# The two wide matmuls of the first attention scores, split into query halves around K's last transposes

## The chip, the cores and the metric

The kernel runs on one core of one Trainium2 chip. The metric is the device time of one execution in microseconds (us). A ratio below is the mean time of one kernel's runs over that of the other's in the same rounds, so it is not quite the ratio of the medians that are quoted.

## The reference, cut to what matters

```python
xn = layernorm(x)                                    # x: 2048 x 640
q = (xn @ wq).reshape(B, Sq, 32, 192)                # 32 heads, head size 192
scores = einsum("bhqd,bhkd->bhqk", q, k_cache) * 192 ** -0.5
o = einsum("bhqk,bhkd->bhqd", softmax(scores), v_cache)
g = silu((silu(x @ w1) * (x @ w3)) @ w2)
return x + (o.reshape(B, Sq, -1) @ wo) * g
```

The kernel walks over 1024 steps of (head, block of 512 queries, pair of key blocks). A step takes scores on PE, exponentials on ACT and the product with V on PE. (PE is TensorE, which multiplies matrices and writes the results to PSUM; ACT is ScalarE, DVE is VectorE, POOL is GpSimd, and SP issues most of the transfers.) The change concerns the very first step, where the pipeline is still being filled.

## The kernel before

The head start brings the first 512 rows of x and K of head 0, normalises x, transposes both on PE, projects the first queries and starts the stream (cut to the end of that function):

```python
    project_first()              # queries of block 0, in two halves of 256 (L391 to L396)
    turn_k0(pk1, 1, (2, 3))      # K's last eight transposes on PE (L271)
    copy_k0(nc.scalar.copy, pk1, 1, 1)     # their copy from PSUM, on ACT (L277)
    scores(0)
    shift_first()                # DVE copies of query halves (L400, L401)
    shift_k0()                   # DVE copy of K rows (L281)
    scores(1)
    ln_stats(1, 0)               # layer norm of the second block, on DVE ...
    ...
    ln_turn_dma(1, 0)            # ... its transposes, by DMA (L360)
```

The first two steps of the scores have a form of their own. Two matmuls on all 128 rows do the work of two rounds, and one round of two half-row matmuls follows:

```python
    if (h, qb) == (0, 0) and p < 2:
        rounds = rounds[2:]
        nc.tensor.matmul(st2[:, 0:512],    lhsT=KW[:, 0, ks], rhs=qA[:], start=True, stop=False)   # L483
        nc.tensor.matmul(st2[:, 512:1024], lhsT=KW[:, 4, ks], rhs=qA[:], start=True, stop=False)   # L484
    for r, (ka, qa, kb, qb2) in enumerate(rounds):
        nc.tensor.matmul(st2[:, 0:512], lhsT=ka, rhs=qa, ...)       # L487, rows 0 to 63
        nc.tensor.matmul(st2[:, 512:1024], lhsT=kb, rhs=qb2, ...)   # L488, rows 64 to 127
    ...                          # exponentials on ACT (L493), in two parts for step 0
```

`swap_halves(0)`, issued when the first block is transposed, copies that block with its partition halves exchanged (xnS). The projection of head 1 (L424, at pair 3 of the first block) uses PE as two row tiles, that is two arrays of 64 of the 128 rows, and its second row tile begins with this copy. The DMA transposes of the second block feed that block's projection of head 0 (L410, at pair 5).

## Time and profile before

| | before |
|---|---|
| time | 1938.26 us (3 runs, 1937.99 to 1938.29) |
| PE busy, granted clock | 99%, 0.999 |
| ACT busy | 61% |
| first exponential starts | 14.08 us |
| waits of the value products for ACT, whole span | 0.6 us |

A timeline row reads: start, busy us, engine, line, operation, output<-input, shapes, count, and in brackets the idle time before it with its releaser. PEld is the loading of PE's weights. A PE row's start is what to read, since the ends of matmuls are modelled.

### The profile page before, as it was taken

To read this page: it belongs to the slowest core of one execution; us is meant where nothing else is said; L and a number is where in the kernel's file an instruction comes from. 1 tells how busy PE (TensorE), PEld (TensorE's weight loads), DVE (VectorE), ACT (ScalarE), POOL (GpSimd) and SP (SyncE) were. 2 spreads that over 40 slices of the span, in tenths; PEclk is the share of its full clock that TensorE was granted. 3 is DMA by queue.
4 is the path that set the end of the run, shared out by engine and by line. 5 is a ranking of instruction groups with operands and counts; after the bars stand their busy time and mean duration, and the time that the engine had idled before them with its cause. 6 is when DMAs were issued, how large, how long until landed. Compare 5 with 4: busy or idle time off the path is not lost.

```text
span 1936.4 us, 59669 instructions
## 1 busy us (share of the span) xinstructions
PE 1926.6 (99%) x27273; PEld 1315.6 (68%) x27281; DVE 654.6 (34%) x997; ACT 1180.0 (61%) x1279; POOL 282.5 (15%) x501
## 2 busy tenths in 40 slices
PE   9999999999999999999999999999999999999998
PEld 6666666666666666666666666666666666577776
DVE  7333333333333333333333333333333334521111
ACT  6677676767676767776777777677767677210000
POOL 3111111111111111111111111111111110000000
PEclk9999999999999999999999999999999999999999
DMA  8643433323333434363434343434334220937783
GB/s 181 129 101 67 98 68 86 84 62 88 59 90 61 100 63 97 68 162 69 101 66 100 69 101 69 101 64 101 69 69 96 58 68 2 260 69 137 151 152 62
DMA packets 394643, 178.98 MB, mean 92 GB/s; under 512 B 341616, under 2 KB 382832, under 8 KB 394384
## 3 DMA queue, kind: packets, MB, share of 16 engines
q1 hardware_dynamic: 371136, 125.32, 31.6%
q0 software_dynamic: 19472, 45.71, 10.0%
q8 instruction: 215, 3.52, 0.8%
q10 hardware_dynamic: 3776, 4.06, 0.7%
q14 instruction: 44, 0.36, 0.1%
HBM read 52.82 MB, written 27.79 MB: 42 GB/s over the span
## 4 chain that ended last, share of the span: by engine, by line
PE 99%; DVE 1%; DMA 0%; ACT 0%; issue 0%; DVEq 0%; ACTq 0%
PE obank L519 35%; PE st L487 34%; PE ps L424 14%; PE ps_s L111 11%; PE ps_f L731 3%; PE ps_gu L705 1%; PE st L488 1%; PE ps L410 0%; DVE stats L316 0%; DMA x_all<-in_A_x_dram 0%; PE ps L391 0%; PE pst L354 0%; PE pk L271 0%; DVE xn L346 0%; ACT pT L493 0%
## 5 line engine op out<-in xcount | busy, mean ns | idle before, releaser
L493 ACT ACTIVATE pT<-st 128x1024 bf16<-128x1024 f32 (+1 forms) x1025 | 1046.1, 1021 | 250.2 <-PE st L488 234.0
L519 PEld LDWEIGHTS <-pT 64*128 64x128 bf16 x16384 | 711.3, 94 | 242.3 <-ACT pT L493 0.6
L519 PE MATMUL obank<-vt,pT 64*128 64x193 bf16 x16384 | 849.7, 243 | 0.0
L487 PE MATMUL st<-qC,KW 64*128 64x512 bf16 x2046 | 605.6, 376 | 0.1
L528 DVE COPY osum<-obank 128x772 f32<-128x772 f32 x128 | 123.1, 962 | 787.1 <-PE obank L519 787.1
L488 PE MATMUL st<-qB,KW 64*128 64x512 bf16 x1024 | 385.0, 376 | 0.0
L487 PE MATMUL st<-qA,KW 64*128 64x512 bf16 x1022 | 384.3, 376 | 0.1
L488 PE MATMUL st<-qC,KW 64*128 64x512 bf16 x1022 | 384.3, 376 | 0.0
L488 PE MATMUL st<-qA,KW 64*128 64x512 bf16 x1022 | 384.3, 376 | 0.0
L487 PEld LDWEIGHTS <-KW 64*128 64x128 bf16 x3068 | 278.5, 94 | 153.7 <-issue 2.1
L424 PE MATMUL ps<-xnT,W 64*128 64x512 bf16 x1280 | 297.2, 376 | 0.0
L424 PE MATMUL ps<-xnS,W 64*128 64x512 bf16 x1280 | 296.0, 376 | 0.0
L488 PEld LDWEIGHTS <-KW 64*128 64x128 bf16 x3068 | 278.5, 94 | 0.5
L377 POOL DMA_DIRECT2D qC<-qA x124 | 65.4, 528 | 1283.0 <-DVE rl_all L535 1268.2
L430 ACT CAST qB<-ps 128x512 bf16<-128x512 f32 x131 | 76.7, 585 | 228.2 <-PE ps L424 222.6
L111 PE MATMUL ps_s<-wo_sb,oT 128*128 128x384 bf16 (+3 forms) x1535 | 208.8, 299 | 0.1
L424 PEld LDWEIGHTS <-W 64*128 64x128 bf16 x2560 | 122.9, 94 | 121.4 <-issue 0.2
L111 PEld LDWEIGHTS <-oT 128*128 128x128 bf16 x1536 | 148.4, 98 | 60.4
L529 DVE TENSOR_TENSOR osum<-osum,obank 128x772 f32<-128x772 f32 x128 | 122.7, 959 | 13.4
L536 DVE TENSOR_TENSOR ostage<-osum,rl_all 128x768 bf16<-128x768 f32 x128 | 122.7, 958 | 6.3 <-DMA o_scr<-ostage 1.9
L465 DVE SCALAR_TENSOR_TENSOR hT<-pt,qB 64x512 bf16<-64x512 bf16 x64 | 43.8, 684 | 197.4 <-ACT pt L464 197.4
L429 DVE CAST qA<-ps 128x512 bf16<-128x512 f32 x131 | 90.6, 692 | 25.3 <-PE ps L410 7.2
(84 smaller groups left out, 621.9 us busy)
## 6 DMA issues: line engine op xcount, KB each, us to landing
o_scr<-ostage SPq DMA_DIRECT2D x16, 1536.0 KB, 10.6
vt<-in_A_v_cache_dram SPq DMA_DIRECT2D x63, 384.0 KB, 5.9
qC<-qA POOLq DMA_DIRECT2D x248, 64.0 KB, 1.9
qC<-qB POOLq DMA_DIRECT2D x124, 64.0 KB, 2.3
wo_sb<-in_A_wo_dram POOLq DMA_DIRECT2D x1, 7680.0 KB, 36.1
W<-in_A_wq_dram POOLq DMA_DIRECT2D x32, 160.0 KB, 3.6
W<-in_B_w_dram POOLq DMA_DIRECT2D x32, 80.0 KB, 3.3
W<-in_A_wq_dram POOLq DMA_DIRECT2D x32, 80.0 KB, 3.0
```

The costliest lines, as they stand in the source:

```text
L111: nc.tensor.matmul(ps[:, 0:w], lhsT=oT[:, k, :], rhs=wo_sb[:, k, c0:c1], start=(k == 0), stop=(k == OC - 1))
L377: nc.gpsimd.dma_start(out=qC[0:64, half, :], in_=qAB[half][64:P, :])
L424: nc.tensor.matmul(ps[:, r * 512:(r + 1) * 512], lhsT=W[rows, j, :], rhs=xs[rows, j // 2, qs], start=(j == 0), stop=(j == 2 * DC - 1))
L429: a = nc.vector.tensor_copy(out=qAB[0][:], in_=ps[:, 0:512])
L430: b = nc.scalar.copy(out=qAB[1][:], in_=ps[:, 512:1024])
L487: nc.tensor.matmul(st2[:, 0:512], lhsT=ka, rhs=qa, start=r == 0 and nr == 3, stop=r == nr - 1)
L488: nc.tensor.matmul(st2[:, 512:1024], lhsT=kb, rhs=qb2, start=r == 0 and nr == 3, stop=r == nr - 1)
L493: nc.scalar.activation(out=pT2[:, c * w:(c + 1) * w], in_=st2[:, c * w:(c + 1) * w], func=ACT.Exp, scale=att_scale)
L519: nc.tensor.matmul(obanks[r][:, j * 256:j * 256 + DH + 1], lhsT=pT2[r * 64:(r + 1) * 64, t * 512 + j * P:t * 512 + (j + 1) * P], rhs=vt[r ...
L528: nc.vector.tensor_copy(out=osum[:], in_=ov[0])
L529: nc.vector.tensor_tensor(out=osum[:], in0=osum[:], in1=ov[1], op=ALU.add)
L536: nc.vector.tensor_tensor(out=ostage[:, qb * 4:qb * 4 + 4, hg * DH:(hg + 1) * DH], in0=osum[:, :, 0:DH], in1=rl.unsqueeze(2).to_broadcast( ...
```

## The change

The intent is to use PE's wait for the second query cast. The two 512-wide matmuls become four of 256. The pair for the first query half runs straight behind the projection, and the pair for the second half behind K's last transposes.

```diff
+    def half_scores():
+        KW, qA, i = loads[0]["KW"], qtiles[0, 0][0][0], early["half"]
+        early["half"] += 1
+        qs = slice(i * 256, (i + 1) * 256)
+        for b, a in enumerate((0, 4)):
+            nc.tensor.matmul(early["st"][:, b * 512 + i * 256:b * 512 + (i + 1) * 256], lhsT=KW[:, a, 0:P], rhs=qA[:, qs],
+                             start=i == 0, stop=False)
...
         project_first()
+        first_scores()
+        half_scores()
         turn_k0(pk1, 1, (2, 3))
         copy_k0(nc.scalar.copy, pk1, 1, 1)
+        half_scores()
         scores(0)
```

`first_scores` only takes the PSUM tile, and the scores of step 0 skip their two wide matmuls where that tile exists. The inserted lines shift the numbering: L484 is now the split matmul, L487/L488 are L507/L508, the exponential L493 is L513, the value product L519 is L539.

More of the change, by code (lines that the diff above doesn't have):

```diff
@@ L469, in _kernel_impl, with first_scores @@
     stream = [(h, qb, p) for h in range(H) for qb in range(NQB) for p in range(NPAIR)]
+    early = {}
+    def first_scores():
+        early["st"] = ps_st.tile([P, 1024], F32, tag="st2", name="st2")
+        early["half"] = 0
+    def half_scores():
[5 more added lines that the diff above has]
+                             start=i == 0, stop=False)
     def emit_scores(h, qb, p):
@@ L476, in emit_scores @@
         ks = slice(p * P, (p + 1) * P)
-        st2 = ps_st.tile([P, 1024], F32, tag="st2", name="st2")
+        st2 = early.pop("st", None)
+        begun = st2 is not None
+        if not begun:
+            st2 = ps_st.tile([P, 1024], F32, tag="st2", name="st2")
         rounds = [(KW[0:64, 0, ks], qA[0:64, :], KW[64:P, 1, ks], qC[64:P, 0, :]),
@@ L482, in emit_scores @@
             rounds = rounds[2:]
-            nc.tensor.matmul(st2[:, 0:512], lhsT=KW[:, 0, ks], rhs=qA[:], start=True, stop=False)
-            nc.tensor.matmul(st2[:, 512:1024], lhsT=KW[:, 4, ks], rhs=qA[:], start=True, stop=False)
+            if not begun:
+                nc.tensor.matmul(st2[:, 0:512], lhsT=KW[:, 0, ks], rhs=qA[:], start=True, stop=False)
+                nc.tensor.matmul(st2[:, 512:1024], lhsT=KW[:, 4, ks], rhs=qA[:], start=True, stop=False)
         nr = len(rounds)
```

## The prediction

> **What bounds the kernel now.** I read the page of the kernel before first (busy shares, slices, chain), then all waits of the weight loads and of PE over the whole span, then the timeline from 8 to 18 us, where the change sits, one engine at a time, and last the chain of work between 12 and 16 us.
>
> ```profile
> PE 1926.6 (99%) x27273; PEld 1315.6 (68%) x27281; DVE 654.6 (34%) x997; ACT 1180.0 (61%) x1279; POOL 282.5 (15%) x501
> PEclk9999999999999999999999999999999999999999
> PE 99%; DVE 1%; DMA 0%; ACT 0%; issue 0%; DVEq 0%; ACTq 0%
> ```
>
> The first line is busy time by engine, the second the granted clock in 40 slices, the third the chain that ended last. TensorE is busy for 99% of the span at full clock and makes up 99% of the chain. The change touches only the first 15 us of 1936, so it can win no more than the waits that stand there. The waits of the weight loads over the whole span (line, releaser, total us, times, longest) say how much that is:
>
> ```profile
> PEld L519 <- ACT pT L493: 0.6, 3, 0.2
> PEld L483 <- ACT qB L394: 0.3, 1, 0.3
> ```
>
> L483 is the first matmul of the first scores, the one that the change splits; L519 multiplies the exponentials by the values, and two of its three waits lie at 14.7 and 15.2 us. So all that is at stake is about 0.3 + 0.4 us, 0.04% of the time. What ends last in this stage is told by the timelines of PE and of ACT (start, us, line, operation, out<-in, count):
>
> ```profile
> 10.15 2.35 PE L391 MATMUL ps<-xnT,W 128*128 128x256 bf16 x20
> 12.33 0.61 PE L271 MATMUL pk<-ident_bf,kn 128*128 128x128 bf16 x8
> 13.10 0.38 PE L483 MATMUL st<-qA,KW 128*128 128x512 bf16 x1 [0.16 <-DVE qA L393]
> 13.63 0.39 PE L487 MATMUL st<-qC,KW 64*128 64x512 bf16 x1
> 14.17 0.38 PE L484 MATMUL st<-qA,KW 128*128 128x512 bf16 x1
> 14.49 0.39 PE L487 MATMUL st<-qC,KW 64*128 64x512 bf16 x1
> ```
> ```profile
> 12.98 1.01 ACT L277 COPY KW<-pk 128x1024 bf16<-128x1024 bf16 x1
> 14.08 1.08 ACT L493 ACTIVATE pT<-st 128x512 bf16<-128x512 f32 x2
> ```
> ```profile
> 12.53 0.42 DVE L393 CAST qA<-ps 128x256 bf16<-128x256 f32 x1 [0.67 <-PE ps L391]
> 12.99 0.29 DVE L396 COPY qC<-qB 64x512 bf16<-64x512 bf16 x1
> ```
>
> The reader is to see two chains that meet at the first exponential, at 14.08. On PE: the projection (L391) ends at 12.50, DVE casts its second half until 12.95, L483 starts at 13.10, L484 one slot later, near 13.31 (its record is missing; its weight load is there at 13.10), L487/L488 at 13.63 until 14.02, and the exponential follows 0.06 us later. On ACT: the eight last turns of K (L271, 12.33 to 12.94) release the copy of K's last part, 12.98 to 13.99; it stands ahead of the exponential in ACT's queue. The chain of waits for 12 to 16 us leads through the PE side. The ACT side is only 0.18 us behind it, as worked out below, and that small margin is what this prediction turns on.
>
> ```profile
> 14.73 0.28 PEld L519 LDWEIGHTS <-pT 64*128 64x128 bf16 x8 [0.15 <-ACT pT L493]
> 15.22 0.28 PEld L519 LDWEIGHTS <-pT 64*128 64x128 bf16 x8 [0.21 <-ACT pT L493]
> ```
>
> These two lines say why the start of the first exponential counts at all: its two halves, 0.59 us each and 0.50 apart, release the first value products, and PE waits for both. From 15.5 us on PE runs without a wait for ACT, and the start of the stream is set.
>
> **What the Trainium skill says.** (1) "TensorE: Matmul & The Clock Gate", Back-to-back issue gap: a warm matmul of N columns takes N/2.4 + 2.5 ns of issue, so 109 ns for 256 columns and 216 for 512. The trace agrees: the 20 matmuls of L391, 256 columns each of 272 ns, take 2.35 us, which is (2.35 - 0.272)/19 = 0.109 each. Splitting a 512-wide matmul in two is thus almost free in streaming. The same page says in its step-by-step part that matmuls stay in program order, so what is put ahead of K's turns delays them. (2) "TensorEngine Tiling (Array Packing)", Key Properties: a change of the tiling mode drains the array. The trace agrees: from L484 (all 128 rows) to L487 (64 rows) is 0.32 us at 14.17, where 0.216 would be the bare issue. (3) "ScalarE: Activation LUTs", What ACT_TABLE_LOAD costs: back-to-back activations overlap by about 93 ns. The trace agrees: the two copies of L277 at 9.57 take 1.94 us together at 1021 ns each, an overlap of 0.10. (4) "PSUM — Partial Sum Buffer", The four PSUM rules: a first matmul with the start flag clears the written marks of its whole bank, so of two groups in one bank only the one issued first may have it, and the other's first write overwrites. The change does it so (start on half 0 only). It costs no time; the value products here already rely on it, two results to a bank.
>
> **The change part by part.**
>
> It removes the two 512-wide matmuls L483 and L484 of the first scores (2 x 0.216 = 0.43 us of issue) and adds four of 256 columns (4 x 0.109 = 0.44 us). The sum of PE's work is unchanged, +0.005 us. Two weight loads are added, 0.098 us each, hidden under matmuls of 0.109 as under L391.
>
> It moves half 0 ahead of K's last eight turns. Its buffer is the one that the casts of the first projection half left at about 11.86, its query columns are from the same cast, and its K columns were copied by 11.50. It should wait for nothing and start at 12.33, where the turns start now. The turns go from 12.33 to 12.33 + 2 x 0.109 = 12.55; their last one starts 7 x 0.056 later, at 12.94, and ends with its 0.219 at 13.16 rather than 12.94. This is the price.
>
> PE's gain: half 1 needs the second cast, which doesn't move (12.95), so it starts at 13.10 like L483 now, and has 0.218 of issue instead of 0.432. L487 then starts at 13.21 + 0.11 + 0.10 for the change of mode = 13.42. It also needs the copy L396, done at 13.28, 0.14 before, which fits the 0.15 that L483 took to follow its cast. So L487/L488 come at about 13.43 rather than 13.63, and end at 13.82 rather than 14.02. By PE alone the exponential would start at 13.88: 0.20 us won.
>
> ACT's loss: its copy of K's last part starts 0.04 after the last turn, so at 13.20 rather than 12.98. The next ACT instruction can start 1.01 - 0.09 = 0.92 later: 13.90 now (which is the margin of 0.18 to 14.08), and 13.20 + 0.92 = **14.12 after**. The first exponential starts at the later of 13.88 and 14.12, so at 14.12, 0.04 us **later** than now. The first value products move from 14.73 to 14.77 and 15.22 to 15.26. The second scores get ready 0.2 us earlier on PE, but only lengthen PE's wait for the exponential. From there everything is shifted by +0.04 us, or less where a DVE chain (the normalisations of the next blocks, which the change leaves where they are) is what PE waits for, as near 34.8 us.
>
> Sum: 0.44 - 0.43 on PE is hidden in a wait, the gain of 0.20 on PE's chain is overtaken by ACT's, and +0.04 is left. 1938.26 + 0.04 = 1938.3 us.
>
> **The rivals.**
>
> PE's chain stays the bound, as the intent of the change is. Then 0.20 us is won: 1938.06. For it: the chain of waits before runs through the PE side and doesn't name ACT. Against it: the copy stands in the same queue as the exponential, 0.18 us from being the bound, and the change delays it by 0.22. A middle way, turns delayed by less because the array overlaps them with something, gives 1938.1 to 1938.3.
>
> A new wait: half 1 comes after the copy of K's last part in program order, and both touch the same K tile. If half 1 were made to wait for the copy (done at 14.21), L487 would start at about 14.60 and the exponential at 15.05, a loss of 0.95: 1939.2. Against it: L483 stands behind the same copy now and started at 13.10, in the middle of it; their columns of K don't overlap.
>
> A shift that grows or vanishes later: a start moved by some hundredths can let a transfer or a DVE step of the first head fall on another side of a PE instruction. Waits there are 0.4 us at most each (the scores at 34.81 for a cast), so some tenths to 1 us either way. The three runs before span 0.3 us, which says that the kernel itself is steady.
>
> **Range and chances.** The main way gives 1938.3, PE's way 1938.06, the false wait 1939.2. To that I add about 1 us to both sides for regrouping in the first head and for another session or chip, which three runs on one chip can't show; that is a guess. Range 1937.0 to 1939.5. Two per cent is 38.8 us, some 50 times all the waits at stake, so within 2% is as good as certain: 0.99, the rest for something that no view shows.
>
> **What would show each step.** Right: two matmuls of 256 columns at about 12.33 and two at 13.10; the turns from 12.55 to 13.16; the ACT copy at 13.20; L487 at 13.43; the first exponential at 14.12, directly behind the copy with no wait for PE; the value products' two waits grown by 0.04 and PE's own time unchanged. Wrong: a first exponential at 13.9 (PE was the bound, or the turns weren't delayed), half 0 later than 12.4 (a wait for its buffer that I haven't seen), L487 later than 13.6 (a false wait for the copy). If these times are as told and the whole differs by more than 0.5 us, the difference comes from later in the kernel, and my step "shifted by +0.04 from there" is what failed.

## The result, and the profile after

The changed kernel took 1938.11 us (median of 6 runs, 1937.93 to 1939.62), the kernel before 1938.13 (6 runs). The ratio is 1.0001, 95% interval 0.9988 to 1.0014: the same time.

The page of the changed kernel, busy time and the chain that ended last:

```profile
PE 1927.4 (100%) x27275; PEld 1316.6 (68%) x27283; DVE 654.3 (34%) x997; ACT 1179.9 (61%) x1279; POOL 282.5 (15%) x501
PE 99%; DVE 0%; ACT 0%; POOL 0%; issue 0%; POOLq 0%; DVEq 0%; ACTq 0%
```

There are two matmuls and two weight loads more. PE's busy time reads 0.8 us more than before, but 0.1 us less in the second pair of profiles below (1927.1 before, 1927.0 after), so that is scatter. The start has to be read closely. In the PE timeline of the changed kernel:

```profile
10.23 2.35 PE L391 MATMUL ps<-xnT,W 128*128 128x256 bf16 x20
12.41 0.38 PE L484 MATMUL st<-qA,KW 128*128 128x256 bf16 x2
12.63 0.61 PE L271 MATMUL pk<-ident_bf,kn 128*128 128x128 bf16 x8
13.09 0.38 PE L484 MATMUL st<-qA,KW 128*128 128x256 bf16 x2
13.41 0.38 PE L507 MATMUL st<-qC,KW 64*128 64x512 bf16 x1
```

And in its ACT timeline:

```profile
13.28 1.01 ACT L277 COPY KW<-pk 128x1024 bf16<-128x1024 bf16 x1 [0.29 <-PE pk L271]
14.18 2.01 ACT L513 ACTIVATE pT<-st 128x512 bf16<-128x512 f32 x3
```

This profile runs 0.08 us late from the first transfer on: the projection L391 starts at 10.23, not 10.15. All times from here on are therefore counted from the start of L391 in the same profile and called relative. For an example, the first exponential is at 14.18 - 10.23 = 3.95 after and 14.08 - 10.15 = 3.93 before.

| relative start, us | before | after |
|---|---|---|
| K's last transposes (PE) | 2.18 | 2.40 |
| their copy (ACT) | 2.83 | 3.05 |
| last round of the first scores (PE) | 3.48 | 3.18 |
| first exponential (ACT) | 3.93 | 3.95 |
| first value product (PE) | 4.59 | 4.61 |

PE is ready 0.30 us earlier, and the exponential comes no earlier. The chain of work from 12 to 16 us in the changed kernel shows what took over:

```profile
12.57 0.22 PE st L484 x2
12.79 0.46 PE pk L271 x8
13.25 0.02 issue
13.28 1.01 ACT KW L277
14.29 0.51 ACT pT L513
14.80 0.05 issue
14.84 1.00 PE obank L539 x16
```

The chain now leads from the inserted half through K's transposes and ACT's copy. Before, it led from the projection through DVE to PE's scores and did not touch ACT's copy:

```profile
12.53 0.42 DVE qA L393
12.99 0.30 DVE qC L396
13.31 0.30 DVE qC L400
13.63 0.39 PE st L487
```

The releaser L400 is inferred here. In the built program L487 waits for L396 alone, done at 13.29, so PE's own order set its start: 13.10, a slot of 0.22 and 0.32 for the last of the wide matmuls give 13.64. PE's gain has become a longer wait for ACT (waits of the weight loads after, to be held against 0.6 before):

```profile
PEld L539 <- ACT pT L513: 0.9, 3, 0.5
```

### The profile page after: what moved, and what is told of

Read it like the earlier page. It is cut to its first block, busy times and chain, and to the rows that moved or that the text cites. A ratio compares the mean times of both kernels' runs of the same rounds, so it can differ in the third digit from the quotient of the medians.

```text
span 1936.2 us, 59673 instructions
## 1 busy us (share of the span) xinstructions
PE 1927.4 (100%) x27275; PEld 1316.6 (68%) x27283; DVE 654.3 (34%) x997; ACT 1179.9 (61%) x1279; POOL 282.5 (15%) x501
## 4 chain that ended last, share of the span: by engine, by line
PE 99%; DVE 0%; ACT 0%; POOL 0%; issue 0%; POOLq 0%; DVEq 0%; ACTq 0%
PE obank L539 35%; PE st L507 34%; PE ps L424 14%; PE ps_s L111 11%; PE ps_f L754 3%; PE ps_gu L728 1%; PE st L508 1%; PE ps L410 0%; PE pk L592 0%; PE ps L391 0%; PE pst L354 0%; PE pk L271 0%; ACT pT L513 0%; ACT KW L277 0%; POOL W L223 0%
## 5 line engine op out<-in xcount | busy, mean ns | idle before, releaser
L513 ACT ACTIVATE pT<-st 128x1024 bf16<-128x1024 f32 (+1 forms) x1025 | 1046.1, 1021 | 250.1 <-PE st L508 234.0
L539 PEld LDWEIGHTS <-pT 64*128 64x128 bf16 x16384 | 711.2, 94 | 242.7 <-ACT pT L513 0.9
L539 PE MATMUL obank<-vt,pT 64*128 64x193 bf16 x16384 | 849.6, 243 | 0.2 <-ACT pT L513 0.2
L507 PE MATMUL st<-qC,KW 64*128 64x512 bf16 x2046 | 605.7, 376 | 0.0
L508 PE MATMUL st<-qB,KW 64*128 64x512 bf16 x1024 | 385.1, 376 | 0.0
L507 PE MATMUL st<-qA,KW 64*128 64x512 bf16 x1022 | 384.4, 376 | 0.1
L508 PE MATMUL st<-qC,KW 64*128 64x512 bf16 x1022 | 384.3, 376 | 0.0
L508 PE MATMUL st<-qA,KW 64*128 64x512 bf16 x1022 | 384.3, 376 | 0.0
L507 PEld LDWEIGHTS <-KW 64*128 64x128 bf16 x3068 | 278.6, 94 | 153.8 <-issue 1.9
L424 PE MATMUL ps<-xnT,W 64*128 64x512 bf16 x1280 | 297.2, 376 | 0.0
L424 PE MATMUL ps<-xnS,W 64*128 64x512 bf16 x1280 | 296.3, 376 | 0.0
L508 PEld LDWEIGHTS <-KW 64*128 64x128 bf16 x3068 | 278.5, 94 | 0.2
L377 POOL DMA_DIRECT2D qC<-qA x124 | 65.4, 528 | 1282.9 <-DVE rl_all L555 1268.2
L424 PEld LDWEIGHTS <-W 64*128 64x128 bf16 x2560 | 122.8, 94 | 121.3
```

The lines of the kernel that those rows point to most:

```text
L377: nc.gpsimd.dma_start(out=qC[0:64, half, :], in_=qAB[half][64:P, :])
L424: nc.tensor.matmul(ps[:, r * 512:(r + 1) * 512], lhsT=W[rows, j, :], rhs=xs[rows, j // 2, qs], start=(j == 0), stop=(j == 2 * DC - 1))
L507: nc.tensor.matmul(st2[:, 0:512], lhsT=ka, rhs=qa, start=r == 0 and nr == 3, stop=r == nr - 1)
L508: nc.tensor.matmul(st2[:, 512:1024], lhsT=kb, rhs=qb2, start=r == 0 and nr == 3, stop=r == nr - 1)
L513: nc.scalar.activation(out=pT2[:, c * w:(c + 1) * w], in_=st2[:, c * w:(c + 1) * w], func=ACT.Exp, scale=att_scale)
L539: nc.tensor.matmul(obanks[r][:, j * 256:j * 256 + DH + 1], lhsT=pT2[r * 64:(r + 1) * 64, t * 512 + j * P:t * 512 + (j + 1) * P], rhs=vt[r ...
```

## The experiments

The theory is that the first exponential starts at the later of two times, PE's last round and ACT's copy, and that the change moved the second by as much as it won on the first. The rivals are that something else in the split holds the exponential, or that the copy does not matter. All kernels gave correct results. For the kernels that were timed, every ratio to the kernel before has an interval of about plus or minus 0.0014 (2.7 us) that holds 1, so the ratios decide nothing here. Runs of one kernel spread too: in the rounds of the first four experiments the kernel before took 1937.77 to 1939.34, five of nine runs at 1939.15 or more.

### Both halves behind the transposes

```diff
-        first_scores()
-        half_scores()
         turn_k0(pk1, 1, (2, 3))
+        first_scores()
+        half_scores()
         copy_k0(nc.scalar.copy, pk1, 1, 1)
         half_scores()
```

> Both halves of the first scores stand behind K's last turns; half 0 fills the wait for the cast. Times are counted from the first matmul of the first projection (L391), where the kernel before has its first exponential at 3.93 us and the changed one at 3.95. My theory (the first exponential starts at the later of PE's scores and ACT's copy of K's last part, and the change delays the copy by 0.22): the turns go back to 2.18, the copy to 2.83, half 1 stays at 2.86 and the last pair of the first scores at 3.18; ACT is free at 2.83 + 0.90 = 3.73, PE ready at 3.63, so the exponential starts at 3.73, the first value product at 4.39 rather than 4.59 or 4.61, and the whole is 0.20 us shorter than the kernel before: 1937.9 for 1938.1. Rival 1 (PE's order is all that counts, ACT's copy doesn't matter): 3.63. Rival 2 (something else that the split brings, a wait for the buffer or for the flags, holds the exponential at about 3.95): no change against the changed kernel.

The PE timeline of this kernel, then its ACT timeline:

```profile
10.37 2.35 PE L391 MATMUL ps<-xnT,W 128*128 128x256 bf16 x20
13.00 0.61 PE L484 MATMUL st<-qA,KW 128*128 128x256 bf16 x4
13.55 0.38 PE L507 MATMUL st<-qC,KW 64*128 64x512 bf16 x1
```
```profile
13.20 1.01 ACT L277 COPY KW<-pk 128x1024 bf16<-128x1024 bf16 x1
14.11 2.01 ACT L513 ACTIVATE pT<-st 128x512 bf16<-128x512 f32 x3
```

The copy is back at 2.83, the last round at 3.18 as in the changed kernel, and the exponential at 3.74 (3.73 expected). The first value product is at 4.40, 0.19 earlier than before. Half 0 now fills exactly the time that PE waited, and delays nothing. The whole time, 1938.04 us (5 runs, ratio 0.9996, 0.9982 to 1.001), can't show 0.2 us.

### The copy on DVE, with the change and without

```diff
-        copy_k0(nc.scalar.copy, pk1, 1, 1)
+        copy_k0(nc.vector.tensor_copy, pk1, 1, 1)
```

In the changed kernel:

> The changed kernel with the copy of K's last part on DVE rather than ACT. My theory: ACT's queue is empty ahead of the exponential, so it starts when PE is ready, 3.18 + 0.39 + 0.05 = 3.62 us after the start of the first projection (3.95 in the changed kernel), the first value product at 4.28. The whole is 0.3 us shorter, unless the 0.68 us more on DVE delay the normalisations that the first head waits for. Rival 1 (the copy isn't what held the exponential): it stays at 3.95. Rival 2 (DVE is the tighter engine here): the exponential comes earlier and the total doesn't follow, or gets worse by up to 0.7.

In the kernel before, as control:

> The kernel before with the copy of K's last part on DVE rather than ACT: the control. My theory says that before, PE was the bound and ACT's copy 0.18 us behind it, so that taking the copy off ACT brings nothing: first exponential at 3.93 us from the start of the first projection, first value product at 4.59, time unchanged. Rival (the copy held the exponential already before): it starts earlier, by up to 0.2.

The ACT row of the changed kernel with this edit, then that of the kernel before with it:

```profile
13.92 2.00 ACT L513 ACTIVATE pT<-st 128x512 bf16<-128x512 f32 x3 [0.87 <-PE st L508]
```
```profile
14.26 2.00 ACT L493 ACTIVATE pT<-st 128x512 bf16<-128x512 f32 x3 [1.18 <-PE st L488]
```

L391 starts at 10.29 and 10.32 here. With the change the exponential moves from 3.95 to 3.63, and its releaser is now PE. Without the change it stays (3.94 for 3.93). The same edit is worth 0.32 us in one kernel and nothing in the other. That shows that the copy binds after the change and didn't bind before it.

The totals don't follow: 1938.29 and 1938.41 us (ratios 0.9998 and 0.9997 to the kernel before in the same rounds). Rival 2 of the first text, that DVE's extra work costs later what was won, is at least partly right. The second block's DMA transposes are issued at 18.74 rather than 18.06 us, and PE waits for what comes of them (L410, below).

### The delay repeated, in two doses

```diff
         half_scores()
+        turn_over(8)            # 36 in the other kernel: idle 128-wide matmuls
         turn_k0(pk1, 1, (2, 3))
```

> The changed kernel with eight idle matmuls of 128 columns more (as in its warm-up) between half 0 and K's last turns: twice as much delay again as half 0 makes. My theory: 8 x 0.056 = 0.45 us on the turns, so the copy at 3.50 and the exponential at 4.40 from the start of the first projection (3.05 and 3.95 in the changed kernel), the first value product at 5.06, and all of it in the whole time: 1938.55. Rival 1 (the exponential isn't bound by turns and copy): less than 0.45 on the exponential. Rival 2 (a shift of the start is taken up by slack in the first head): the exponential moves, the total doesn't.

> The changed kernel with 36 idle matmuls of 128 columns between half 0 and K's last turns: a delay large enough to be read in the whole time. My theory: 36 x 0.056 = 2.0 us on turns, copy (5.06 us from the start of the first projection), exponential (5.96) and first value product (6.62), and as PE is the bound from there on, the whole time 2.0 us longer, 1940.1. Rival (slack in the first head, where PE waits for DVE at 20 to 40 us, takes up part of it): between 0 and 1.5 us longer; then a gain of some tenths at the first exponential needn't reach the total either.

Copy and exponential on ACT with 8 (L391 at 10.28), then with 36 (L391 at 10.40):

```profile
13.77 1.01 ACT L277 COPY KW<-pk 128x1024 bf16<-128x1024 bf16 x1 [0.74 <-PE pk L271]
14.68 2.01 ACT L513 ACTIVATE pT<-st 128x512 bf16<-128x512 f32 x3
```
```profile
15.46 1.01 ACT L277 COPY KW<-pk 128x1024 bf16<-128x1024 bf16 x1 [2.30 <-DVE stats L316]
16.36 2.01 ACT L513 ACTIVATE pT<-st 128x512 bf16<-128x512 f32 x3
```

(The copy waits for PE's transposes in both. The releaser L316 in the second is a wrong inference: the transposes there run from 14.81 to 15.42.) Copies at 3.49 and 5.06, exponentials at 4.40 and 5.96, value products at 5.06 and 6.62: all as expected to 0.01 us. A delay on K's transposes is a delay on the first exponential, one for one. The 36-matmul kernel took 1940.15 us (5 runs within 0.11), against 1938.34 for the kernel before in its rounds (1937.97 to 1939.07, so no run of the one reaches the other; ratio 1.0009, 0.9995 to 1.0022). By the medians 1.8 of the 2.0 us arrived at the end. The small dose took 1938.42 (ratio 0.9998), within the spread of its neighbours, so the 0.45 us expected in its time is neither shown nor refuted.

### Both halves behind and the copy on DVE

This combines the first and the second edit.

> Both halves behind K's last turns and the copy of K's last part on DVE. My theory: with the copy off ACT's queue the delay of the turns no longer counts, so this is as the changed kernel with the copy on DVE: exponential at 3.62 us from the start of the first projection, first value product at 4.28; whole time within 0.05 us of that kernel's, 0.3 below the kernel before. Rival (the delayed turns hurt in another way than through the copy): this one is faster by up to 0.2.

The exponential is at 3.63 and the value product at 4.28, the same as with the copy on DVE alone. So the delayed transposes hurt through ACT's copy and in no other way that shows here. The time is a miss: 1939.08 us, not 0.3 below but 0.7 above the kernel before (1938.34 in the same rounds, ratio 1.0002, not told apart). The profile says where it went. L391 starts at 10.71 here, 0.3 us or more later than in any other profile, and the rest is waiting. PE rows of the projection of head 1 in this kernel:

```profile
19.10 0.38 PE L424 MATMUL ps<-xnT,W 64*128 64x512 bf16 x1
20.12 0.39 PE L424 MATMUL ps<-xnS,W 64*128 64x512 bf16 x2 [0.64 <-DMA xnS<-xnT]
```

PE reaches the projection early (relative 8.39) and then waits 1.02 us from the first row tile to the second, for the transfer of the swapped halves. That led to a look at the same place in the first profile of the kernel before and of the changed one:

```profile
18.84 0.38 PE L424 MATMUL ps<-xnT,W 64*128 64x512 bf16 x1
19.05 0.39 PE L424 MATMUL ps<-xnS,W 64*128 64x512 bf16 x2
```
```profile
18.95 0.38 PE L424 MATMUL ps<-xnT,W 64*128 64x512 bf16 x1
18.96 0.59 PE L424 MATMUL ps<-xnS,W 64*128 64x512 bf16 x2
```

Before, the second tile came 0.21 us late; after, both start together. Is that the change's doing? Two more profiles were taken to find out.

### The same two kernels again

> The kernel before, profiled once more: a measure of how far two profiles of one kernel differ. Expected: first exponential 3.93 us and first value product 4.59 after the start of the first projection again, to 0.02; the start of that projection itself (10.15 in the first profile) and the landing of the swapped halves (8.90 after it) may differ by some tenths, as they come from transfers, and if my reading is right the wait of the second row tile for the swap (0.2 us in the first profile) changes with the landing.

> The changed kernel, profiled once more. Expected: copy at 3.05, first exponential at 3.95, first value product at 4.61 after the start of the first projection again, to 0.02; start of that projection and landing of the swapped halves by some tenths from the first profile (10.23 and up to 8.73 after it). If the landing comes later than 8.72, the changed kernel shows the same wait of the second row tile as the kernel before, and the 0.2 us between the two first profiles at the second projection of head 0 is not the change's doing.

These are single runs, so their state is unknown; the clock was 1.0 and 0.999. Everything up to the first value product repeats within 0.01 us (3.93 and 4.58; 3.05, 3.95 and 4.61). The second row tile of the changed kernel doesn't repeat:

```profile
19.01 0.38 PE L424 MATMUL ps<-xnT,W 64*128 64x512 bf16 x1
19.50 0.39 PE L424 MATMUL ps<-xnS,W 64*128 64x512 bf16 x2
25.29 2.32 PE L410 MATMUL ps<-xnT,W 128*128 128x512 bf16 x9
```

This time it waited 0.49 us. The slower transfer of the swapped halves took 7.2 us from issue to landing in the first profile of this kernel and 7.8 in this one. So the 0.2 us that seemed to speak for the change is the scatter of a transfer.

### The projection of head 1 one step later, and a load issued later

The next two kernels start from the one with both halves behind.

```diff
-        if h == 0 and qb == 0 and p == 3:
+        if h == 0 and qb == 0 and p == 4:
             project(1, 0)
```

> Both halves behind K's turns, as in the first experiment, and the projection of head 1 one step later (pair 4 rather than pair 3). Its second row tile reads the copy of the normalised input with its halves swapped, whose transfer landed in the runs so far 8.5 to 9.4 us after the start of the first projection, where PE comes to it at 8.4 to 8.7 (9.2 and 10.7 in the two delayed kernels). My theory, formed after the first experiments: what is won at the first exponential is lost again to this landing and to that of the transposes of the second block (which the second projection of head 0 waits for, at 14.4 to 14.8), so the gain doesn't reach the whole. With the projection later, PE comes to it at about 9.8 and doesn't wait for the swap: no step between its two row tiles. The second projection of head 0 still waits for the transposes, at 14.4 from the start of the first projection as in the first experiment, so the whole stays within 0.15 us of that kernel: 1938.0. Rival (the swap was the only thing that took the gain): second projection at 14.2 or earlier and the whole 0.2 us shorter.

A miss. The wait for the swap is gone, but a new one stands in its place: PE comes to the transposes of the second block (L354) before DVE has normalised it. PE row, 0.73 us idle:

```profile
21.05 0.81 PE L354 MATMUL pst<-ident_bf,xn 128*128 128x128 bf16 x10 [0.73 <-DVE xn L346]
```

L410 came at 15.31 rather than 14.4, and the time was 1938.96 us (5 runs, 1938.89 to 1941.37; ratio 1.0007, 0.9994 to 1.0021). The old place of the projection had covered DVE's work, so this run doesn't settle what the swap alone is worth.

```diff
-        load_x(2)
         project_first()
...
         scores(1)
+        load_x(2, queue=nc.scalar)
```

> Both halves behind K's turns, as in the first experiment, and the load of the third block of the input (640 KB) issued behind the second exponential, at about 16.1, rather than at 13.4 us: less traffic beside the swapped halves. In all eleven profiles so far the time of the run is 1913.2 to 1913.4 us more than the start of the second projection of head 0, which follows the landing of the second block's second transpose by 0.2 us. My theory (what a run takes is set by these landings, and they by the traffic on the transfer engines): the swap lands at 8.2 us after the start of the first projection or earlier, PE's two row tiles start together at about 8.5, and the gain of 0.2 is kept up to there; the late load now lies beside the transposes, so they may land as late as now or later (14.3 to 15.0), and the time follows the second projection's start plus 1913.3 either way. Rival (landing doesn't depend on that load): swap at 8.5 to 9.2 as before, nothing else changed. A loss is likely if the load lands after 21.9, where DVE reads it.

ACT's queue issued the load at 14.82, a little before the second exponential. The two row tiles started together (18.85, relative 8.51), and the slower half of the swap took 7.0 us, landing at relative 8.4 rather than the 8.2 that was expected. That is the shortest of the profiles compared (7.0 to 7.9), but by 0.1, which is less than the scatter just seen. L410 came at 14.30, the time was 1937.86 us (ratio 0.9999, 0.9986 to 1.0013). It is the lowest median and not told apart from the kernel before, so whether the load's traffic matters stays open.

### The profiles side by side

The second projection of head 0 (L410) is the last place where they differ. All but the last two columns are relative to L391; "tile 1/tile 2" are the starts of the two row tiles of L424.

| kernel | L391 at | first exponential | value product | L424 tile 1/tile 2 | L410 | that run's time | time minus L410's own start |
|---|---|---|---|---|---|---|---|
| before | 10.15 | 3.93 | 4.59 | 8.69/8.90 | 14.69 | 1938.20 | 1913.36 |
| before, again | 10.28 | 3.93 | 4.58 | 8.69/8.99 | 14.73 | 1938.22 | 1913.21 |
| after | 10.23 | 3.95 | 4.61 | 8.72/8.73 | 14.48 | 1937.93 | 1913.22 |
| after, again | 10.29 | 3.95 | 4.61 | 8.72/9.21 | 15.00 | 1938.51 | 1913.22 |
| both behind | 10.37 | 3.74 | 4.40 | 8.51/8.53 | 14.37 | 1938.08 | 1913.34 |
| after, copy on DVE | 10.29 | 3.63 | 4.28 | 8.39/8.75 | 14.80 | 1938.29 | 1913.20 |
| before, copy on DVE | 10.32 | 3.94 | 4.59 | 8.70/9.08 | 14.86 | 1938.48 | 1913.30 |
| after, 8 idle | 10.28 | 4.40 | 5.06 | 9.17/9.17 | 14.88 | 1938.41 | 1913.25 |
| after, 36 idle | 10.40 | 5.96 | 6.62 | 10.73/10.73 | 16.38 | 1940.06 | 1913.28 |
| both behind, copy on DVE | 10.71 | 3.63 | 4.28 | 8.39/9.41 | 15.15 | 1939.24 | 1913.38 |
| both behind, later projection | 10.33 | 3.74 | 4.40 | 11.46/11.46 | 15.31 | 1938.96 | 1913.32 |
| both behind, later load | 10.34 | 3.74 | 4.40 | 8.51/8.51 | 14.30 | 1937.86 | 1913.22 |

The last column is the find. Over twelve profiles whose times differ by 2.2 us, what comes after L410 takes 1913.2 to 1913.4 us. All but 0.2 us of what these profiled runs differ by, win, loss and scatter alike, is made by the start of L410, 27 us into the span at the latest.

From the value product to L410 the profiles need 9.76 us at the least (36 idle matmuls, where the transfers have landed long before) and 10.87 in the kernel with both halves behind and the copy on DVE, whose order of work is otherwise the usual one. The excess is waiting: for the swap, and at L410 itself. L410's first weight load waits for two transfers in the built program, and the semaphores are those that the two DMA transposes (L360) count up. In ten of the twelve profiles the load starts 0.1 us after the second of them landed. In the first profile after, for instance, the second was issued at 18.06 + 2.64 - 1.20 = 19.50 and landed 5.1 us later, at 24.6, and the load starts at 24.68. In the other two, PE comes 3.2 us (36 idle matmuls) and 2.4 us (later projection) after that landing. In these two the transfer was also quicker, 3.9 and 3.6 us from issue to landing against 4.8 to 5.6 in the ten, and the transfers of head 1's queries (L377) were issued after the landing rather than before it. So this landing seems to depend on when PE gets to the projection of head 1; why was not tested.

## Why the prediction was right or wrong

The time was right: 1938.3 told, 1938.11 measured, in the range, and the class was the near-certain one. The sign of +0.04 is not confirmed by the times: 0.02 below the kernel before, with runs 1.7 us apart. The range (1937.0 to 1939.5) is wider than the scatter of the kernel before alone (1937.77 to 1939.34), so that the time fell into it says little about the mechanism; the traces have to.

- **Half 0 starts without a wait and delays the transposes by 0.22.** Right: transposes at 2.18 before and 2.40 after.
- **The copy at 13.20, the exponential at 14.12.** Right: with L391 at 10.15 these are relative 3.05 and 3.97; measured 3.05 and 3.95. Copy and exponential start 0.90 apart, not 0.92. The overlap of 0.09 that was taken from the Trainium skill's page for pairs of activations holds for a copy followed by an exponential too, and was 0.11.
- **PE's gain of 0.20.** Right in kind, too small: it was 0.30 (3.48 to 3.18). The step that failed is "it starts at 13.10 like L483 now". Half 1 started at relative 2.86, not 2.95. The reason stands in the instruction listing of the built program (before, then after; the wait for DVE before is an instruction of its own just ahead of the weight load, counted to it here):

```
233 L483 Ldweights KW [waits DVE_49,Activation_49]
234 L483 Matmult st_312<-qA,KW 128x512 [waits Activation_49]

237 L484 Ldweights KW
238 L484 Matmult st_303<-qA,KW 128x256 [waits DVE_49]
```

Before, the weight load itself waits for DVE and ACT, so load and matmul both follow the cast: 13.10, 0.15 after the cast's end. After, half 0's weight load has done that waiting, half 1's weights load early, and only the matmul waits: 13.09, 0.06 after the cast's end at 13.03. That this is the cause follows from the listing and the two lags; no run took it away alone. From half 1 to the last round it is 0.32 in the changed kernel and also with 8 idle matmuls, where L396 was done 0.48 earlier than the round, so PE's own order suffices for that stretch. But in the changed kernel DVE's copy L396, which the round needs too, ended only 0.05 before it (13.36, then 13.41): half 1 any earlier would have met that copy.

- **"The chain of waits for 12 to 16 us leads through the PE side."** Loosely read: as shown above it runs over DVE's cast and copies to L487. That ACT's copy is not in it is right, and that is what the sum needed.
- **ACT's loss overtakes PE's gain.** Right, and shown: by the chain after, by the copy on DVE (0.32 us in one kernel, nothing in the other), by the two doses, and by both halves behind (0.21 us earlier than the changed kernel).
- **"From there everything is shifted by +0.04 us", or less for a DVE chain near 34.8.** This step failed. There are two later meetings, at 18.9 and 24.7 us, where PE comes within tenths of a transfer's landing, and the two profiles of the changed kernel differ by 0.6 us in the first of these landings and by 0.5 us in L410's start. I had checked the waits for ACT only, and taken the rest for a PE without waits. The wait of 0.21 at L424 was in the profile before, in a row labelled "issue" that I passed over, and busy time hid it because the first tile's matmul was still counted. Of the rivals, the one that a shift "grows or vanishes later" by a transfer falling on another side of a PE instruction is what the traces show.
- **A false wait of half 1 for the copy.** Absent: half 1 started at 13.09, the copy at 13.28.

So a gain of tenths at the first exponential is partly spent waiting at the landings, while a delay beyond them passes on. The first value product came 0.19 earlier than before with both halves behind. At L410 this kernel is 0.32 earlier than the first profile before and 0.11 earlier than the first after, but these two differ by 0.21 although their value products start within 0.02. I therefore claim no gain for that kernel, although its first exponential is earlier beyond doubt.

The 1.6 us spread of the runs of the kernel before was not traced run by run. The one profile of such a long run (1939.24) had both a late L391 (10.71) and a late swap, which suggests but doesn't show that the other long runs come from late transfers.

## What to carry to other kernels

Before filling one engine's wait, look for who else waits on the work that the filler pushes back. Here eight transposes fed a copy that stood in the same queue as the next consumer, with 0.18 us to spare, and a filler of 0.22 us in front of them undid what it won; behind them it would have cost nothing. Take two profiles of the same kernel before crediting a change with some tenths in a stage fed by transfers, and find the point after which the profiles agree, since it bounds where a difference can come from.

## What the Trainium skill lacked or had wrong

- "TensorEngine Tiling (Array Packing)", Key Properties, says that tiles operate independently. They don't when one waits: matmuls of both row tiles stand in one order. With both halves behind and the copy on DVE, the second tile's wait for the swap held the first tile's next matmul too, whose own operand had landed 2.2 us before: it started at 20.12 with the second tile's first, 1.02 us after the first tile's first rather than a slot of 0.22. In the kernel before, where the wait was 0.21, just a slot, the two tiles then stayed one slot out of step until the next scores had ended. "TensorE: Matmul & The Clock Gate", Step-by-step, does say that matmuls stay in order.
- "TensorE: Matmul & The Clock Gate", Step-by-step, tells when weight loads are pulled ahead, but not what a semaphore wait on the weight load itself costs: the matmul followed its operand by 0.15 us with such a wait and by 0.06 where only the matmul waited.
- "ScalarE: Activation LUTs" gives the overlap of about 93 ns for activations; a copy of 128x1024 from PSUM followed by an exponential overlapped by 0.11 us here. The page doesn't speak of that mix.
- I found on no page how far the landing of one transfer scatters between runs of one kernel: the slower half of the swap of 2 x 320 KB landed 7.0 to 7.9 us after its issue, 7.2 and 7.8 in two runs of the same program.
